# First layer by seven block products instead of eight, and the layers' side work ordered by a list scheduler

## The chip, the core and the metric

The kernel runs on one core of a Trainium2 chip. Four compute engines work side by side, each through its own instructions in order: TensorE (PE in the profile; its weight loads are a row of their own, PEld), VectorE (DVE), ScalarE (ACT) and GpSimd (POOL). SyncE (SP) issues most of the DMA transfers. The metric is the device time of one execution in microseconds, lower is better; the time before is the median of three runs, 629.89 us (629.33 to 630.28).

## The reference

```python
scores = (q @ k.T) / sqrt(64)                  # 4 batches x 12 heads, 448 x 448
scores = cap * tanh(scores / cap)              # cap = 30
attn = exp(scores - max); attn = attn / (attn.sum() + 1e-9)
x = (attn @ v)  -> (1792 tokens, 768)
h = x @ w_in                                   # 768 x 2048
g = where(h > 0, h, exp(min(h, 0)) - 1)
out = g @ w_out                                # 2048 x 768
```

All values are float32. The kernel writes each float32 factor as a high part in TensorE's `float32r` format plus a low part, and takes three products: high x high, high x low and low x high.

## The kernel before

Attention. Twelve rounds (`Attention.run`) handle 24 pairs of heads. Per round ScalarE runs seven `tanh` and seven `exp` passes over 128x896 elements, TensorE the scores, values and row sums, VectorE the casts, sums and evictions. `normalise` writes x, transposed: 128 of the 768 features by 448 tokens for each pair. `Tokens.high` and `Tokens.low` split x. The order of all this is written out by hand, as times in `AT` and `END`.

Layers. The 1792 tokens are cut into `BLOCKS` of 512, 512, 512 and 256. The 2048 hidden features are taken in `NR` = 8 rounds of two tiles of 128 (`FT` = 2). For each of the 32 units (round r, block t), `Moe.first` computes two hidden tiles (per tile 6 feature chunks x 3 products = 18 matmuls), and `Moe.second` multiplies the two activated tiles by the second weights into six output tiles (6 x 2 x 3 = 36 matmuls), in pairs of two PSUM banks. TensorE's order is: first layer of the next unit, then second layer of this one. So each unit has 72 matmuls, each round 288.

Work beside TensorE. `elu` (lines 240 to 256) takes a hidden tile through ScalarE `exp` (L245), VectorE `min` and add (L246), VectorE maximum and add (L249, reads PSUM), ScalarE copy into the high part (L254) and VectorE subtraction into the low part (L255). `finish` (L306) adds each pair of output tiles from PSUM to the accumulator in SBUF. In round 0 ScalarE copies them instead (L290). The weights arrive packed; `Weights.steps` unpacks each of the 32 tiles of 128x768 with three VectorE passes (L128 to L130), one ScalarE pass (L140), VectorE (L144), a GpSimd addition (L147), a ScalarE copy into the high part (L154) and a VectorE subtraction into the low part (L158). In the layers this runs as a string of steps at fixed places of each unit (`WRUN`), and mostly one step right behind the other.

Queues and buffers. VectorE, ScalarE and GpSimd run their instructions in the order written. PSUM has two single banks, `pv0` and `pv1`, for hidden tiles, and three pairs for outputs. SP's queue carries the weight loads (768 KB each) and, at the end, the output (512 KB each, smaller ones last).

Of the kernel before, what the change touches and what calls it, by code (L numbers as in the profile page):

```python
# [17 lines left out]
P = 128  # L18
# [9 lines left out]
NW = 2 * NF  # L28
CP = 64
WSTEPS = 5  # L30
# [9 lines left out]
def pieces(b):  # L40

    out = []
    for t, (t0, n) in enumerate(BLOCKS):
        lo, hi = max(t0, b * S), min(t0 + n, (b + 1) * S)
        if lo < hi:
            out.append((t, lo - t0, lo - b * S, hi - lo))
    return out

# [23 lines left out]
END = {  # L72
    "invert": 2.95, "spread": 2.97, "normalise": 3.2, "unit0": 0.1, "xh": 0.2, "elu0": 1.55, "unit0b": 1.6,
    "xl": 2.9, "elu1": 3.0,
    "weights": (1.0, 2.96, 3.25),
}
# [6 lines left out]
class Weights:  # L83
# [4 lines left out]
    def __init__(self, nc, pool, pre, w):  # L88
        self.nc, self.pool, self.pre, self.w = nc, pool, pre, w
        self.late = self.now = None  # L90
        self.scalar = False
        self.raw, self.split = {}, {}
        self.nraw = self.nmid = 0

    def buffer(self, k, n, width, dtype):

        if self.late and k % 2:
            return self.late.tile([P, width], dtype, name=f"{n}{k}", tag=n, bufs=1)
        if n == "wq":
            return self.pool.tile([P, width], dtype, name=f"{n}{k}", tag=n, bufs=1)  # L100
        at = 0 if n == "wr" else 2 * DM
        return self.pre[:, at : at + width].bitcast(dtype)

    def ahead(self):

        self.load(self.nmid + (2 if self.now is None else 1) - self.nraw)

    def load(self, n=1):
        for k in range(self.nraw, min(self.nraw + n, NW)):
            t = self.buffer(k, "wr", 2 * DM, I32)  # L110
# [4 lines left out]
    def steps(self):  # L115

        nc = self.nc
        k = self.nmid
        if k >= NW:
            return  # L120
        self.nmid += 1
        raw = self.raw.pop(k)
        high = raw.rearrange("p (n w) -> p n w", w=2)[:, :, 1]
        low = raw.bitcast(U16).rearrange("p (n w) -> p n w", w=4)[:, :, 1]
        v = self.buffer(k, "wv", DM, F32)
        q = self.buffer(k, "wq", DM, I32)
        vi = v.bitcast(I32)
        nc.vector.tensor_single_scalar(out=vi, in_=high, scalar=0x7FFFFFFF, op=ALU.bitwise_and)  # L128
        nc.vector.tensor_scalar_max(v, v, TINY)
        nc.vector.tensor_scalar(  # L130
# [8 lines left out]
        if self.scalar:  # L139
            nc.scalar.activation(out=q, in_=low, func=AF.Copy, scale=2.0**-13)  # L140
        else:
            nc.vector.tensor_scalar_mul(q, low, 2.0**-13)
        yield
# [5 lines left out]
        v = v.rearrange("p (c n) -> p c n", c=6)  # L149
        pool, n = (self.pool, 4) if k % 6 < 4 else (self.late, 2)  # L150
        h = pool.tile([P, 6, P], F32R, name=f"wh{k}", tag="wh", bufs=n)
        l = pool.tile([P, 6, P], F32R, name=f"wl{k}", tag="wl", bufs=n)
        if self.scalar:
# [5 lines left out]
        self.split[k] = (h, l)  # L159

    def run(self, n):

        for _ in range(n):
            if self.now is None:
                self.now = self.steps()
            if next(self.now, self) is self:
                self.now = None

    def get(self, f, second):
        return self.split[f // FT * 2 * FT + f % FT + FT * second]  # L170


class Tokens:


    def __init__(self, nc, pool, early):
        self.nc, self.pool, self.early, self.late = nc, pool, early, None
        self.x, self.parts = {}, {}

    def new(self, p):  # L180
        self.x[p] = self.pool.tile([P, BANK], F32, name=f"x{p}", tag="x", bufs=NPAIR + 1)[:, :S]
        return self.x[p]

    def split(self, p, t):
        self.high(p, t)
        self.low(p, t)

    def piece(self, p, t):
        return next((o, at, n) for k, o, at, n in pieces(p // PPB) if k == t)

    def high(self, p, t, vector=False):
        c = p % PPB
        o, at, n = self.piece(p, t)
        if (t, c) not in self.parts:
            n0 = BLOCKS[t][1]
            if t == NB - 1:
                both = self.late.tile([P, 2, n0], F32R, name=f"xb{c}", tag="xb", bufs=PPB)
                self.parts[t, c] = [both[:, 0], both[:, 1]]
            else:
                pool, k = (self.early, 2 * PPB) if t < 2 else (self.late, PPB)  # L200
                xh = pool.tile([P, BANK], F32R, name=f"xh{t}_{c}", tag="xh", bufs=k)[:, :n0]
                self.parts[t, c] = [xh, None]
        out, x = self.parts[t, c][0][:, o : o + n], self.x[p][:, at : at + n]
        if vector:
            self.nc.vector.tensor_copy(out=out, in_=x)
        else:
            self.nc.scalar.activation(out=out, in_=x, func=AF.Copy)

    def low(self, p, t):
        c = p % PPB  # L210
        o, at, n = self.piece(p, t)
        part = self.parts[t, c]
        if part[1] is None:
            part[1] = self.pool.tile([P, BANK], F32R, name=f"xl{t}_{c}", tag="x", bufs=NPAIR + 1)[:, : BLOCKS[t][1]]
# [568 lines left out]
```

## Time and profile before

| | us |
|---|---|
| median of three runs | 629.89 (629.33 to 630.28) |
| profiled execution, its own time | 629.86 |
| its span, first to last instruction | 627.6 |
| PE busy in the span | 618.4 (99%) |
| DVE busy | 444.4 (71%) |
| ACT busy | 282.9 (45%) |
| POOL busy | 62.3 (10%) |

A busy PE is not PE at its peak, because matmuls overlap: the distance between the starts of two matmuls (the pitch) tells what one costs in a stream. A share over the whole span mixes attention (to about 160 us) and the layers (from there on), so the views below are taken by stretch.

### The profile page before, as it was taken

What the parts mean: (1) busy time and instruction counts of PE and PEld (TensorE: products, weight loads), DVE (VectorE), ACT (ScalarE), POOL (GpSimd) and SP (SyncE); (2) the same over time, 40 slices, a digit from 0 to 9 for tenths busy, and PEclk for the clock granted to TensorE, in tenths of its full rate; (3) what the DMA queues carried; (4) which work ended last, traced back from release to release, by engine and by line L of the source; (5) the groups of instructions that cost most, each with busy time, mean ns of one, the idle gap of its engine ahead of it and who ended that gap; (6) DMA issues with size and microseconds to landing.
All of it is one profiled execution on the core that took longest, in us unless ns stands there. A gap on an engine that the chain in (4) does not pass through costs nothing.

```text
span 627.6 us, 8706 instructions
## 1 busy us (share of the span) xinstructions
PE 618.4 (99%) x3410; PEld 461.6 (74%) x3410; DVE 444.4 (71%) x672; ACT 282.9 (45%) x399; POOL 62.3 (10%) x40
## 2 busy tenths in 40 slices
PE   8999999999999999999999999999999999999996
PEld 3444444444788788888888888888888888888885
DVE  5898999998877556766776766576767577484443
ACT  6999999999445542222312222322332123121110
POOL 0010010010101211210111211111111121110000
PEclk9999999999999999999999999999999999999999
DMA  5546457561141311210211122111111122000224
GB/s 184 174 152 208 135 164 216 134 192 54 37 131 50 101 52 50 81 72 7 95 50 51 57 66 80 51 50 51 51 51 50 51 76 76 1 2 0 101 101 156
DMA packets 26227, 54.30 MB, mean 87 GB/s; under 512 B 9538, under 2 KB 13634, under 8 KB 26178
## 3 DMA queue, kind: packets, MB, share of 16 engines
q1 hardware_dynamic: 25890, 53.27, 26.7%
q8 instruction: 29, 0.48, 0.3%
q10 hardware_dynamic: 288, 0.39, 0.2%
q14 instruction: 20, 0.16, 0.1%
HBM read 47.97 MB, written 5.59 MB: 85 GB/s over the span
## 4 chain that ended last, share of the span: by engine, by line
PE 84%; DVE 9%; ACT 2%; DMA 2%; issue 1%; SPq 1%; POOL 1%; DVEq 0%; POOLq 0%; ACTq 0%
PE o L231 11%; PE o L232 11%; PE o L233 11%; PE h L231 11%; PE h L233 11%; PE h L232 11%; PE pv L414 7%; PE s L372 5%; DVE u L448 2%; PE sum L458 2%; PE pv L427 1%; PE s L389 1%; DVE xl L216 1%; DVE qkl L367 1%; DMA pre<-in_w_dram 1%
## 5 line engine op out<-in xcount | busy, mean ns | idle before, releaser
L231 PE MATMUL o<-gh,wh 128*128 128x512 f32 (+1 forms) x380 | 138.3, 364 | 0.4 <-ACT acc L290 0.4
L232 PE MATMUL o<-gl,wh 128*128 128x512 f32 (+1 forms) x380 | 138.2, 364 | 0.0
L233 PE MATMUL o<-gh,wl 128*128 128x512 f32 (+1 forms) x380 | 138.1, 363 | 0.0
L231 PE MATMUL h<-xh,wh 128*128 128x512 f32 x288 | 112.3, 390 | 0.1
L232 PE MATMUL h<-xl,wh 128*128 128x512 f32 x288 | 112.1, 389 | 0.0
L233 PE MATMUL h<-xh,wl 128*128 128x512 f32 x288 | 112.1, 389 | 0.0
L306 DVE TENSOR_TENSOR acc<-o,acc 128x1024 f32<-128x1024 f32 (+1 forms) x83 | 89.1, 1089 | 10.3 <-PE o L233 10.3
L254 ACT ACTIVATE gh<-e 128x512 fp32r<-128x512 f32 (+1 forms) x64 | 37.0, 579 | 103.8 <-DVE e L249 103.8
L245 ACT ACTIVATE e<-h 128x512 f32<-128x512 f32 (+1 forms) x64 | 34.6, 540 | 103.5 <-PE h L233 99.7
L231 PEld LDWEIGHTS o<-gh,wh 128*128 128x128 f32 x380 | 71.7, 189 | 12.4 <-ACT acc L290 0.9
L233 PEld LDWEIGHTS o<-gh,wl 128*128 128x128 f32 x380 | 71.7, 189 | 11.3
L232 PEld LDWEIGHTS o<-gl,wh 128*128 128x128 f32 x380 | 71.8, 189 | 11.2
L405 ACT ACTIVATE s<-s 128x896 f32<-128x896 f32 x84 | 76.6, 911 | 5.5 <-PE s L389 3.5
L407 ACT ACTIVATE p<-s 128x896 f32<-128x896 f32 x84 | 77.2, 919 | 2.7
L255 DVE TENSOR_TENSOR gl<-e,gh 128x512 fp32r<-128x512 f32 (+1 forms) x64 | 41.8, 653 | 41.3 <-ACT gh L254 40.6
L147 POOL TENSOR_TENSOR pre<-pre,wq 128x768 int32<-128x768 int32 x18 | 35.5, 1975 | 339.3 <-DVE pre L144 301.1
L246 DVE TENSOR_SCALAR e<-e 128x512 f32<-128x512 f32 (+1 forms) x64 | 26.4, 413 | 55.6 <-ACT e L245 55.5
L231 PEld LDWEIGHTS h<-xh,wh 128*128 128x128 f32 x288 | 54.1, 188 | 12.6 <-DVE e L249 0.9
L233 PEld LDWEIGHTS h<-xh,wl 128*128 128x128 f32 x288 | 54.1, 188 | 11.3
L232 PEld LDWEIGHTS h<-xl,wh 128*128 128x128 f32 x288 | 54.1, 188 | 10.9
L414 PE MATMUL pv<-p,vf 128*64 128x448 f32 x276 | 59.5, 552 | 0.2
L249 DVE SCALAR_TENSOR_TENSOR e<-h,e 128x512 f32<-128x512 f32 (+1 forms) x64 | 40.0, 625 | 2.2
(86 smaller groups left out, 722.9 us busy)
## 6 DMA issues: line engine op xcount, KB each, us to landing
pre<-in_w_dram SPq DMA_DIRECT2D x18, 768.0 KB, 4.5
wr<-in_w_dram SPq DMA_DIRECT2D x14, 768.0 KB, 4.2
raw<-in_qk_dram SPq DMA_DIRECT2D x22, 448.0 KB, 4.1
vf<-in_v_dram SPq DMA_DIRECT2D x23, 256.0 KB, 4.1
rb<-rec SPq DMA_DIRECT2D x48, 112.0 KB, 3.0
out_dram<-acc SPq DMA_DIRECT2D x9, 512.0 KB, 2.8
den<-sums SPq DMA_DIRECT2D x48, 1.8 KB, 1.9
out_dram<-acc SPq DMA_DIRECT2D x2, 256.0 KB, 3.5
```

The lines of the kernel that those rows point to most:

```text
L147: nc.gpsimd.tensor_tensor(out=vi, in0=vi, in1=q, op=ALU.add)
L231: mm(acc, wh[:, m, :], ph, start=first, stop=False)
L232: mm(acc, wh[:, m, :], pl, start=False, stop=False)
L233: mm(acc, wl[:, m, :], ph, start=False, stop=last)
L245: nc.scalar.activation(out=ev, in_=h, func=AF.Exp)
L249: nc.vector.scalar_tensor_tensor(out=ev, in0=h, scalar=0.0, in1=ev, op0=ALU.max, op1=ALU.add)
L254: nc.scalar.activation(out=gh, in_=ev, func=AF.Copy)
L255: nc.vector.tensor_tensor(out=gl, in0=ev, in1=gh.bitcast(F32), op=ALU.subtract)
L306: self.nc.vector.tensor_tensor(out=o, in0=s, in1=o, op=ALU.add)
L405: self.nc.scalar.activation(out=s, in_=s, func=AF.Tanh, scale=self.con.tanh_scale)
L407: self.nc.scalar.activation(out=pt, in_=s, func=AF.Exp, scale=self.con.exp_scale)
L414: self.nc.tensor.matmul(out[o, :S], w[j], x[j], **flags)
```

## The change

In rounds 1 to 7 the first layer for the last 1024 tokens is computed by Strassen's scheme. Two hidden tiles x 1024 tokens x 768 features is a 2x2 by 2x2 product of blocks (each 128 hidden features, 384 features deep, 512 tokens wide). Eight block products of 9 matmuls (3 chunks x 3 products) become seven. For it, four sums of weight quarters are formed each round (`Weights.sum`, `form_high`, `form_low`), and four sums of token quarters once, in place of x (`Tokens.combine`, 12 operations of 128x512). These are split into high and low parts in twelve chunks; nine chunks of 512 KB are sent to DRAM, and each round fetches 12 chunks back into a ring of three buffers (`NEXT` says which form follows which product). The seven products leave PSUM through one ScalarE copy (`keep`) and seven VectorE additions (`add`), which also combine them.

`BLOCKS` becomes 384, 384, 512, 512; the first two blocks are computed as before. The elu becomes two ScalarE passes (`Relu` with scale -1, `Exp` with scale -1) and one VectorE pass instead of one and two. The weights' first pass (L128) moves to ScalarE (`Abs`), and all raw tiles use one buffer. x becomes one tile, whose space later holds the accumulators.

The order of the work is no longer written by hand. `Plan` holds threads of `Step`s with an engine, a duration, a due time, and what each needs, gives, takes and frees. It runs them in simulated time; at each point the engine that is free first takes the step that is due first, and the instructions are emitted in this order. TensorE's order is fixed by `plan_products`. GpSimd and VectorE are independent engines in the plan. The normalisation of the last five pairs, with the DMAs around it, is dealt out by the plan too (`plan_rest`).

The core of the diff:

```diff
-BLOCKS = [(t, min(BANK, B * S - t)) for t in range(0, B * S, BANK)]
...
-WRUN = ((2, 2, 1, 1), (2, 2, 1, 1), (2, 1, 1, 1), (1, 1, 1, 1))
+BLOCKS = ((0, 384), (384, 384), (768, BANK), (768 + BANK, BANK))
...
+LAG = {"p": 0.15, "s": 0.1, "v": 0.06, "g": 0.1, "d": 1.8, None: 0.0}
+FREE = {"p": 0.0, "s": -3.7, "v": -0.75, "g": 1.2, "d": 0.0}
+NORMAL = 5
+NEXT = {6: (3, 0), 7: (4, 0), 4: (1, 0), 5: (2, 1)}
+USES = {6: 2, 7: 3, 4: 4, 5: 1}
+TAKES = {6: 2, 7: 3, 5: 1, 3: 4}
...
+        if scalar:
+            self.v[k] = self.v_buffer(k)
+            nc.scalar.activation(out=self.v[k], in_=high.bitcast(F32), func=AF.Abs)
+            yield
+            q = self.quotient(k)
+            nc.scalar.activation(out=q, in_=low, func=AF.Copy, scale=2.0**-13)
+            yield
+            v = self.v[k]
...
+    def sum(self, r, k):
+
+        a, b = (self.v[2 * FT * r + i].rearrange("p (j n) -> p j n", j=2) for i in range(FT))
+        x, y, op, o = (
+            (b[:, 0], b[:, 1], ALU.add, b[:, 1]),
+            (a[:, 0], b[:, 0], ALU.subtract, b[:, 0]),
+            (b[:, 1], a[:, 0], ALU.subtract, a[:, 0]),
+            (a[:, 1], a[:, 0], ALU.subtract, a[:, 1]),
+        )[k]
+        self.nc.vector.tensor_tensor(out=o, in0=x, in1=y, op=op)
...
+        self.nc.scalar.activation(out=h, in_=self.fresh[r, k], func=AF.Copy)
...
+        self.nc.vector.tensor_tensor(out=l, in0=self.fresh[r, k], in1=h.bitcast(F32), op=ALU.subtract)
...
+    def combine(self, i, k):
+
+        x = [[self.block(HC * j + i, PAIR + n) for n in range(2)] for j in range(2)]
+        o, a, b = (
+            (x[0][0], x[0][1], x[0][0]),
+            (x[0][1], x[1][1], x[0][1]),
+            (x[1][1], x[1][1], x[0][0]),
+            (x[1][0], x[1][0], x[1][1]),
+        )[k]
+        self.nc.vector.tensor_tensor(out=o, in0=a, in1=b, op=ALU.subtract)
...
+        self.nc.scalar.activation(out=t[:, 0], in_=self.form(n, i), func=AF.Copy)
...
+        self.nc.vector.tensor_tensor(out=l, in0=self.form(n, i), in1=h.bitcast(F32), op=ALU.subtract)
...
+        self.nc.sync.dma_start(out=d, in_=self.whole.pop((n, i)).bitcast(F32))
...
+        self.nc.sync.dma_start(out=t.bitcast(F32), in_=self.forms[n, i])
...
+            engine = min(first, key=lambda e: first[e])
+            now = first[engine]
+            due, _, step, head = min(
+                ((step.due, k, step, head) for k, (start, step, head) in enumerate(able)
+                 if step.engine == engine and start <= now),
+                key=lambda e: e[:2],
+            )
...
+        for step in order:
+            if step.f is not None:
+                step.f(*step.a)
...
+        self.nc.scalar.activation(out=e, in_=self.h[k], func=AF.Relu, scale=-1.0)
+        self.nc.scalar.activation(out=e, in_=e, func=AF.Exp, scale=-1.0)
...
+            out=e, in0=e, scalar=-1.0, in1=self.h.pop(k), op0=ALU.add, op1=ALU.max
...
+        a, b = {
+            1: ((0, 0), (0, 0)), 2: ((0, 1), (1, 0)), 3: (4, (1, 1)),
+            4: ((1, 1), 4), 5: (1, 1), 6: (2, 2), 7: (3, 3),
+        }[n]
...
+        u, out = {6: ("c1", "u2"), 7: ("u2", "u3"), 4: ("u3", "c"), 2: ("c1", None), 3: ("u2", None), 5: ("u3", None)}[n]
...
+        for t in range(2, NB):
+            self.plan_second(0, t - 2)
+            first(0, t)
+        self.plan_second(0, NB - 2)
+        for r in range(1, NR):
+            self.begun[r] = self.clock
+            for n in (1, 6):
+                if r == 1 and n == 1:
+                    first(r, 0)
+                self.plan_block(n, r)
+            if r > 1:
+                first(r, 0)
+            self.plan_second(r - 1, 3)
+            self.plan_block(7, r)
+            first(r, 1)
+            self.plan_second(r, 0)
+            for n in (4, 2, 3):
+                self.plan_block(n, r)
+            self.plan_second(r, 1)
+            self.plan_block(5, r)
+            self.plan_second(r, 2)
+        self.plan_second(NR - 1, 3)
+        self.plan.thread(*self.pe)
+
...
+        order = [(n, i) for i in range(HC) for n in (1, 4)] + [(n, i) for n in (3, 2) for i in range(HC)]
...
```

`plan_opening` gives the due times of the splits and sums in round 0: block 1 from -3.0, block 2 from 8, block 3 from 20, the sums from 24, the twelve chunks from 26 in steps of 1.4, in us from the start of the second hidden tile.

## Rows read from the trace of the kernel before

**Rows 1.** The page: granted TensorE clock in 40 slices, tenths of full speed.

```profile
PEclk9999999999999999999999999999999999999999
```

**Rows 2.** Stretches: start:end length, busy us (x instructions) per engine, clock, DMA share, GB/s.

```profile
323.20:380.80 57.60, 57.60 (x290) 49.15 (x289) 40.59 (x58) 15.28 (x25) 7.39 (x4) 1.00 0.17 55
...
163.80:210.00 46.20, 45.75 (x217) 38.29 (x218) 32.83 (x67) 22.28 (x42) 5.60 (x3) 1.00 0.30 89
```

**Rows 3.** TensorE in order of time: start, us, engine, line, tiles.

```profile
598.25 0.39 PE L231 MATMUL o<-gh,wh 128*128 128x512 f32 x1
...
598.48 0.39 PE L232 MATMUL o<-gl,wh 128*128 128x512 f32 x1
```

**Rows 4.** VectorE by line and shape, 170 to 627 us: xcount, busy us, mean ns.

```profile
L306 DVE TENSOR_TENSOR acc<-o,acc 128x1024 f32<-128x1024 f32 x63 | 75.9, 1218 | 9.4 <-PE o L233 9.4
...
L249 DVE SCALAR_TENSOR_TENSOR e<-h,e 128x512 f32<-128x512 f32 x47 | 32.5, 692 | 1.6
...
L158 DVE TENSOR_TENSOR wl<-pre,wh 128x768 fp32r<-128x768 f32 x15 | 14.3, 956 | 29.1 <-ACT wh L154 29.1
...
L144 DVE SCALAR_TENSOR_TENSOR pre<-pre 128x768 int32<-128x768 int32 x15 | 14.2, 946 | 0.0
...
L129 DVE TENSOR_SCALAR pre<-pre 128x768 f32<-128x768 f32 x14 | 7.8, 561 | 0.5
...
L249 DVE SCALAR_TENSOR_TENSOR e<-h,e 128x256 f32<-128x256 f32 x16 | 6.8, 425 | 0.6
```

**Rows 5.** ScalarE by line and shape, the same stretch.

```profile
L254 ACT ACTIVATE gh<-e 128x512 fp32r<-128x512 f32 x47 | 29.7, 632 | 72.7 <-DVE e L249 72.7
...
L245 ACT ACTIVATE e<-h 128x512 f32<-128x512 f32 x46 | 27.4, 597 | 88.8 <-PE h L233 88.8
...
L154 ACT ACTIVATE wh<-pre 128x768 fp32r<-128x768 f32 x15 | 12.7, 844 | 62.1 <-POOL pre L147 33.6 <-PE h L232 28.6
...
L140 ACT ACTIVATE wq<-pre 128x768 int32<-128x768 uint16 x14 | 12.6, 899 | 0.0
```

**Rows 6.** All groups by line: the one table load of ScalarE.

```profile
L636 ACT ACT_TABLE_LOAD x1 | 1.3, 1283 | 1.1 <-PEq L772 1.1
```

**Rows 7.** Timelines of POOL and DVE around two GpSimd additions.

```profile
346.15 1.85 POOL L147 TENSOR_TENSOR pre<-pre,wq 128x768 int32<-128x768 int32 x1 [14.24 <-DVE pre L144]
...
346.69 1.59 DVE L246 TENSOR_SCALAR e<-e 128x512 f32<-128x512 f32 x1 [0.69 <-ACT e L245]
...
374.09 2.35 DVE L306 TENSOR_TENSOR acc<-o,acc 128x1024 f32<-128x1024 f32 x2
...
374.31 1.85 POOL L147 TENSOR_TENSOR pre<-pre,wq 128x768 int32<-128x768 int32 x1 [13.19 <-DVE pre L144]
```

**Rows 8.** What VectorE waited for, 208 to 540 us: total us, times, longest.

```profile
DVE e L246 <- ACT e L245: 39.8, 29, 3.2
...
DVE wl L158 <- ACT wh L154: 34.7, 17, 5.9
...
DVE gl L255 <- ACT gh L254: 30.3, 47, 0.7
```

**Rows 9.** Chain that ended last, in order of time: start, us, what.

```profile
89.71 0.91 PE pv L427 x8
...
102.25 0.91 PE pv L427 x8
...
153.49 0.91 PE pv L427 x8
```

**Rows 10.** VectorE by line and shape, 0 to 170 us.

```profile
L216 DVE TENSOR_TENSOR xl<-x,xh 128x64 fp32r<-128x64 f32 x6 | 1.0, 208 | 0.0
```

**Rows 11.** DMA issues: xcount, KB each, median us from issue to landing.

```profile
wr<-in_w_dram SPq DMA_DIRECT2D x14, 768.0 KB, 4.2
...
out_dram<-acc SPq DMA_DIRECT2D x2, 256.0 KB, 3.5
...
out_dram<-acc ACTq DMA_DIRECT2D x1, 128.0 KB, 2.6
```

More of the change, by code (lines that the diff above doesn't have):

```diff
@@ L177, in __init__ @@
         self.nc, self.pool, self.early, self.late = nc, pool, early, None
-        self.x, self.parts = {}, {}
+        self.all = pool.tile([P, NC, B * S], F32, name="x")
+        self.parts = {}
+        self.forms, self.ring, self.whole = {}, {}, {}
     def new(self, p):
[L181 to L189, printed above, removed]
@@ L209, in low @@
[L209 to L214, printed above, removed]
-        h, l = (a[:, o : o + n] for a in part[:2])
-        self.nc.vector.tensor_tensor(out=l, in0=self.x[p][:, at : at + n], in1=h.bitcast(F32), op=ALU.subtract)
+        b, c = divmod(p, PPB)
+        return self.all[:, c, b * S : b * S + S]
@@ new lines, in block, with high @@
+    def block(self, c, t, n=1):
+        t0, width = BLOCKS[t]
+        return self.all[:, c : c + n, t0 : t0 + width] if n > 1 else self.all[:, c, t0 : t0 + width]
+    def high(self, c, t, vector=False):
+        width = BLOCKS[t][1]
+        if t == 1:
+            part = self.parts[1, c]
+        elif t == PAIR + 1 and c < HC:
+            part = [self.spare[:, (2 * c + i) * BANK : (2 * c + i + 1) * BANK] for i in range(2)]
+        else:
+            pool, n, bufs = (self.early, "x", NC) if t == 0 else (self.late, "b", 3 * HC)
+            part = [pool.tile([P, width], F32R, name=f"x{i}{t}_{c}", tag=n + i, bufs=bufs) for i in "hl"]
+        self.parts[t, c] = part
+        if vector:
+            self.nc.vector.tensor_copy(out=part[0], in_=self.block(c, t))
+        else:
+            self.nc.scalar.activation(out=part[0], in_=self.block(c, t), func=AF.Copy)
@@ new lines, in plan_first @@
+    def plan_first(self, r, t, i):
+        f, end = r * FT + i, 0.0
+        bank = ("h", r, t, i)
+        for c in range(NC):
+            more = {"takes": ("bank", bank)} if c == 0 and (r, t) != (0, 0) else {}
+            needs = [("w", self.tile(f, 0))] + [("x", t, c)] * (t > 0)
+            if c == NC - 1:
+                more["gives"] = ("p", r, t, i)
+            end = self.product(self.hidden, r, t, i, (c,), n=3, width=BLOCKS[t][1], needs=needs, **more)
+        frees = (bank,) if (r, t) != (0, 0) else ("h0",) if i else ()
+        self.plan_elu(r, t, i, end, needs=(("p", r, t, i),), frees=frees)
@@ L726, in path, with pool @@
[L726 to L729 removed]
+                def pool(kind, on=ctx, **more):
+                    return on.enter_context(tc.tile_pool(name=f"{kind}{tag}", bufs=1, **more))
+                x.dr = dr = pool("dr", space=DRAM)
+                tail, at, heads = (ctx.enter_context(ExitStack()) for _ in range(3))
+                back = pool("tail", tail, side="right")
```

687 lines of the change are left out of this document (497 added, 190 removed).

## Prediction

> **What bounds the kernel now.** I read three views, in this order. The stretches come first. In one round's length of the layers, 323.2 to 380.8 us, TensorE is busy 57.60 of 57.60 us with 290 matmuls (a round has 288), at clock 1.00 [rows 2], which is the upper of its two levels, 2.4 GHz; it stays there in every slice [rows 1]. A busy TensorE proves little by itself, so the second view is TensorE in order of time. Two matmuls 512 wide start 0.23 us apart although each is shown as 0.39 us long [rows 3]. One round of 57.6 us gives the finer figure: 216 matmuls of 512 and 72 of 256, on average 448 wide, make 57.6 / 288 = 0.200 us each. That is 448 / 2400 = 0.1867 plus 0.0133 us. So 512 wide costs 0.2267 us, 256 wide 0.120, and 384 wide, which the trace does not show, 0.1733 by the same line. TensorE is at its column rate: in the layers, a matmul taken away is time taken away, as long as nothing else comes late. The third view is the other engines in the same round: VectorE 40.59 us, ScalarE 15.28, GpSimd 7.39 [rows 2]. VectorE has 17 us of room, and most of this is waiting in its own order: 105 us in the 332 us from 208 to 540, behind ScalarE passes [rows 8].
>
> **What TensorE loses and keeps.** Before, the two wide blocks of the new cut would cost 2 tiles x 2 blocks x 6 chunks x 3 = 72 matmuls a round in the first layer. Seven products of 9 are 63. Nine matmuls of 512 go, in seven rounds: 63 x 0.2267 = 14.28 us. The new cut itself (384, 384, 512, 512) keeps the number of matmuls and the mean width 448, so it costs nothing. A new round is 57.6 - 2.04 = 55.56 us of TensorE.
>
> **VectorE and ScalarE in a new round.** VectorE, by rows 4, with 128x384 taken as 0.56 us between 0.425 (256) and 0.692 (512): four weight tiles lose L128 and keep 0.561 + 0.561 + 0.946 + 0.956 = 3.02 each, 12.1 us. Four weight sums and four low parts of 384 are 8 x 0.56 = 4.5. The elu keeps its maximum and low part, four tiles of 512 and four of 384: 8 x 0.69 + 8 x 0.56 = 10.0. Accumulation is 6 x 1.218 and 6 of 768 wide at about 0.95, 13.0. Seven additions of products are 4.8. The sum is 44.4 of 55.56 us (80%), against 40.6 of 57.6 (70%). ScalarE [rows 5]: tiles 4 x (0.84 + 0.90 + 0.84) = 10.3, four high parts of weight sums 2.0, three passes for eight elu tiles 13.2, the kept product 0.6, together 26 us (47%). `Relu` and `Abs` are not in the trace. The nearest rows are `Exp` (0.597) and `Copy` (0.632) of the same shape; the upper bound is one table load of 1.283 each [rows 6], which with loads to and fro at 12 places a round would be 31 us more and fill ScalarE. I take no load, because `Exp`, `Tanh` and `Copy` already share the one load of the whole trace. The Trainium skill, "ScalarE: Activation LUTs", section "Table sets: the hidden batching unit", says that cheap functions such as relu and abs lie in every set; no row here shows it.
>
> Where could a round lose? Two single PSUM banks serve eleven tiles a round. Products 4, 2, 3 follow each other at 2.04 us; product 3 needs the bank of 4, so VectorE has 2.04 us for one addition of 0.69 and whatever it is in the middle of (up to 1.22). That fits, with 0.1 us to spare. I put 0.1 us on each of seven rounds, 0.7 us in all, bounds 0 and 4.
>
> **The opening (round 0).** Here the new work is bunched. From the start of the second hidden tile, TensorE reaches product 6 of round 1, the first that needs sums, after 3.12 + 6.24 + 6.24 + 8.16 + 6.24 + 8.16 + 8.16 + 6.24 + 2.04 = 54.6 us. Until then VectorE must do: low parts of x 6 x 0.56 + 12 x 0.69 = 11.6; five normalisations and the row sums 4.1; eight elu tiles 4 x 1.12 + 4 x 1.38 = 10.0; token sums 12 x 0.69 = 8.3; their low parts 8.3; one weight low part 0.96 and two tiles 6.0; weight sums and one low part 2.8. That is 52.1 us. Back to back, two accumulations of 1.218 take 2.35 [rows 7], so each of some 60 operations gives back about 0.08, and 47 to 48 us remain. That leaves 6 to 7 us for waiting. In the like stretch before, 163.8 to 210 us, VectorE stood idle 46.2 - 32.8 = 13.4 us [rows 2], by waits of the kinds of rows 8, at steps placed right behind the one they wait for; the new order can put other ready work between.
>
> GpSimd takes some of the rest. While its addition ran (346.15 to 348.00), a VectorE pass that began at 346.69 took 1.59 us and ended at 348.28, where even the two-operand maximum of this width takes 0.692 [rows 4, 7]. While another ran (374.31 to 376.16), two accumulations that read PSUM went at full speed [rows 7]. So an addition holds up some VectorE work by 0.9 to 1.85 us. Three fall into the opening (2.7 to 5.6 us), four into each round (3.6 to 7.4), and the plan counts the two engines as independent. The Trainium skill, "SBUF — State Buffer", section "Who interferes with whom", states the rule: a VectorE operation with two SBUF inputs, or in a two-port mode, and a GpSimd operation that reads SBUF exclude each other for a whole instruction. By that rule nearly all new work (sums, low parts) is of the exposed kind; the two cases in the trace agree with it.
>
> The balance is 47.5 + 4 = 51.5 us of work for 54.6, so 3 us for waits. I take a TensorE stall of 2.0 us, bounds 0 (waits mostly gone) and 9 (waits as before: 51.5 + 13.4 - 54.6 = 10, of which a little is hidden behind product 6).
>
> **DMA.** Each round now fetches 12 chunks of 512 KB beside four weight loads. A load of 768 KB lands in 4.2 us [rows 11], so three chunks, even one after the other at that price, land in 12.6 us. The shortest gap is from product 4 to product 5: 2 x 2.04 + 6.24 = 10.3 us, plus 1.4 from chunk one's release to the end of product 4, plus 1.4 until chunk three is used: 13.1. I take 0 us; with a weight load ahead in SP's queue the group would be 3.7 us late.
>
> **Attention.** Up to its eighth round a round takes 102.25 - 89.71 = 12.54 us, the last four (153.49 - 102.25) / 4 = 12.81 [rows 9]. These four lose 1.1 us in all. The new cut takes VectorE work out of them: the 64-token pieces of x out of three of these rounds (two splits of 0.2 us per round and part [rows 10]). I take -0.8 us, bounds 0 and -1.1.
>
> **The end.** The last addition is 512 wide instead of 256: 0.69 for 0.425 us. The last transfers are 256 KB (3.5 us) instead of 128 KB (2.6) [rows 11]. Together 0.3 to 1.2; I take +0.7.
>
> **The sum.** The profiled execution took 629.86 us (span 627.6 and 2.3 around it), the median of the runs is 629.89, so one base serves: 629.86 - 14.28 - 0.8 + 2.0 + 0.7 + 0.7 = 618.2 us.
>
> **The rivals.**
> 1. VectorE's opening is late by the full 9 to 10 us, with the additions of GpSimd in it, and rounds lose up to 4: 629.86 - 14.28 + 9 + 4 + 0.7 = 629, or half of it 622 to 625. For: work of 51.5 for 54.6 us, tight. Against: waits of the old kind are what a scheduler removes.
> 2. By the rule on shared ports alone: the rounds too lose what each addition holds up. 44.4 + 7.4 = 51.8 us stays under 55.56, so the rounds hold, and the opening takes its 5.6 instead of 4: 620 us.
> 3. A fetch group queued behind a weight load is late by 3.7 us in each of seven rounds: 618.2 + 26 = 644, or 622 for one round. Against: a weight load fits between the groups.
> 4. Slower than before: VectorE keeps waiting in its order as now. Rows 8 give 105 us in 332, that is 18.2 us a round. 44.4 + 18.2 = 62.6 us would make VectorE the bound of each round, 5.0 above the old 57.6: 629.86 + 35 = 665 us. It decides from 13.2 us of waits a round. Against: waits for `exp` and for high parts end when other ready work is put in front.
> 5. The change doesn't do what it says: 384-wide matmuls cost as much as 512. Then 8 x 144 x 0.053 = 61 us are lost. Against: a straight line through 256 and 512.
>
> **How the numbers follow.** A measurement of this kernel can tell about 0.2% (1.3 us) from no change. Forecast with its small terms, 614.5 to 621: 0.65 (rival 2's 620 us lies in it, with 0.15 of this). Rival 1: 0.18, two thirds of it below 626. Rival 3: 0.06. Rival 4: 0.08. Rival 5 and others: 0.03. The low end is all terms at their best: 629.86 - 14.28 - 1.1 + 0.3 = 614.8, rounded to 614.5. The high end, 626, takes in 0.65 + 0.12 + 0.03 = 0.80. Faster by over 0.2%: 0.65 + 0.16 + 0.04 + 0.01 = 0.86. Within: 0.03. Slower: 0.11.
>
> **What would show it right or wrong.** In the changed kernel's stretches a middle round should take 55.6 to 55.9 us, with TensorE at 63 matmuls fewer in all, VectorE near 44 us busy (less what overlaps) and its waits well under 13. What TensorE waits for should be a few us in all, most of it at the first matmuls of product 6 in round 1, released by VectorE or ScalarE work on the sums. VectorE passes over SBUF should be 1 to 2 us long beside GpSimd additions. It would be wrong if TensorE waits in every round (banks, or a DMA into the ring), if a table load stands beside `Relu`, or if the granted clock fell to its lower level after a stall.

## The result, and the profile after

The changed kernel takes 623.45 us (median of 4 runs, 622.50 to 623.72) where the kernel before took 629.61 beside it (4 runs): a ratio of 0.9898, 95% interval 0.9881 to 0.9915. The forecast was 618.2 us with a range of 614.5 to 626. Sign and range held; 5 us of the gain are missing. The profiled execution of after took 623.72 us, its span is 621.9.

The stretches come first, as in rows 2: start:end, length, busy us (instructions) of PE, PEld, DVE, ACT and POOL, granted clock, DMA share, GB/s. The first line has the length of a round and lies in round 2 and the start of round 3, the second is round 1, the third a piece of the opening with the start of round 1.

```profile
276.50:332.44 55.94, 55.94 (x281) 50.32 (x280) 46.20 (x62) 25.56 (x42) 8.05 (x5) 1.00 0.49 169
...
209.26:272.36 63.10, 58.34 (x280) 51.28 (x279) 50.87 (x74) 38.08 (x60) 11.82 (x6) 0.97 0.64 225
...
171.00:221.00 50.00, 47.05 (x234) 41.74 (x232) 47.37 (x73) 36.19 (x62) 6.13 (x3) 1.00 0.46 164
```

The starts of TensorE's rounds lie at 209.26 (round 1), 272.36, 328.30, 384.23, 440.16, 496.10 and 552.03 us. So round 1 takes 63.10 us and every later one 55.93; a round before took 57.64 by the same landmarks. In rounds 2 to 7 TensorE waits for nothing. In the layers it waits four times in the whole trace (us in total, times, longest):

```profile
PE o L402 <- ACT wv L118: 1.8, 1, 1.8
PE m L402 <- issue: 1.7, 1, 1.7
...
PE m L402 <- DVE e L435: 1.2, 1, 1.2
PE h L402 <- DVE e L435: 0.8, 1, 0.8
```

The wait of the last line, at 163.76 us (1.0 us lost), was there before the change as well. The other three lie in round 1. Here they are one by one, in order of time (start, us, engine, line, tiles, idle before and releaser). The first is at product 1:

```profile
212.38 0.62 ACT L276 ACTIVATE t<-x 128x512 fp32r<-128x512 f32 x1
212.90 1.01 ACT L467 ACTIVATE x<-o 128x1024 f32<-128x1024 f32 x1
213.91 0.63 ACT L276 ACTIVATE t<-x 128x512 fp32r<-128x512 f32 x1
214.44 0.89 ACT L121 ACTIVATE wq<-pre 128x768 int32<-128x768 uint16 x1
215.24 0.47 ACT L430 ACTIVATE e<-h 128x384 f32<-128x384 f32 x1
...
216.30 0.55 DVE L435 SCALAR_TENSOR_TENSOR e<-e,h 128x384 f32<-128x384 f32 x1
...
216.91 0.50 PE L402 MATMUL m<-xh,wh 128*128 128x512 f32 x1 [1.21 <-DVE e L435]
```

Product 1 needs the PSUM bank of the first hidden tile of round 1. That tile was complete at about 212.4 us; its bank is freed by the maximum at L435, which ends at 216.85. In between ScalarE, in its fixed order, did 2.8 us of other work (two chunks' high parts, a copy out of PSUM, a weight step) before the tile's first pass at 215.24. The second wait follows at product 6:

```profile
217.89 2.11 POOL L148 TENSOR_TENSOR wv<-wv,wq 128x768 int32<-128x768 int32 x1 [13.46 <-DVE wv L145]
...
218.24 2.18 DVE L449 TENSOR_TENSOR gl<-e,gh 128x384 fp32r<-128x384 f32 x1
...
218.86 0.39 PE L404 MATMUL m<-xh,wl 128*128 128x512 f32 x1
...
220.34 0.54 DVE L435 SCALAR_TENSOR_TENSOR e<-e,h 128x384 f32<-128x384 f32 x1
...
220.98 0.47 PE L402 MATMUL m<-t,forms 128*128 128x512 f32 x1 [1.74 <-issue]
```

The subtraction at L449 took 2.18 us beside the GpSimd addition; without one such a pass takes 0.55. The maximum that frees the bank of the second hidden tile stood behind it, ended at 220.88, and TensorE went on at 220.98. The trace names no releaser ("issue"); that it is this bank is read from the order and the 0.1 us between the two. The third wait, for a pair of banks of the second layer, and what came after it:

```profile
254.99 1.85 POOL L148 TENSOR_TENSOR wv<-wv,wq 128x768 int32<-128x768 int32 x1 [7.54 <-DVE wv L145]
...
255.34 1.92 DVE L211 TENSOR_TENSOR forms<-pre,forms 128x384 fp32r<-128x384 f32 x1
...
261.39 0.95 DVE L472 TENSOR_TENSOR x<-o,x 128x768 f32<-128x768 f32 x1
...
262.48 0.47 PE L402 MATMUL o<-gh,wh 128*128 128x512 f32 x1 [1.81 <-ACT wv L118]
...
263.09 0.63 PE L404 MATMUL o<-gh,wl 128*128 128x512 f32 x1
263.52 0.63 PE L402 MATMUL o<-gh,wh 128*128 128x512 f32 x1
```

The pair's tiles were complete at about 254.2 us; the accumulation at L472 that frees them ended at 262.34, behind a queue that again held a stretched pass (1.92 us). The ScalarE pass that the row names (L118) had nothing to do with these banks. After the wait eight matmuls stand 0.43 us apart instead of 0.23. The granted clock had fallen to the lower of the two levels, 1.2 GHz, with TensorE busy (columns as in the stretches above):

```profile
262.95:266.30 3.35, 3.35 (x9) 2.57 (x9) 3.31 (x6) 1.42 (x3) 0.00 (x0) 0.50 0.61 213
```

From the wait's end at 262.48 to 266.43 us the slow matmuls cost 1.7 us more than the pitch of 0.228. The three waits cost 1.39, 1.89 and 1.97 us; with the slow matmuls that is 6.9 of the 7.17 us by which round 1 is longer than its followers. The rest stands at the first matmuls behind the first two waits.

Four lines of the page and of the lines' view, for the terms of DMA and the table load (columns as in rows 11 and 6). All twelve chunks are sent to DRAM, not the nine that the description of the change names:

```profile
t<-form SPq DMA_DIRECT2D x81, 512.0 KB, 5.3
pre<-in_w_dram SPq DMA_DIRECT2D x32, 768.0 KB, 5.7
...
form<-t SPq DMA_DIRECT2D x12, 512.0 KB, 3.9
...
L1098 ACT ACT_TABLE_LOAD x1 | 1.3, 1283 | 1.1 <-PEq L1249 1.1
```

And the chain that ended last, in attention, to be read against the last line of rows 9:

```profile
152.50 0.91 PE pv L866 x8
```

### The profile page after: what moved, and what is told of

Its sections match the earlier page's. It is cut to its first block, busy times and chain, and to the rows that moved or that the text cites. A ratio compares the mean times of both kernels' runs of the same rounds, so it can differ in the third digit from the quotient of the medians.

```text
span 621.9 us, 8936 instructions
## 1 busy us (share of the span) xinstructions
PE 608.4 (98%) x3347; PEld 473.6 (76%) x3347; DVE 491.0 (79%) x684; ACT 365.3 (59%) x527; POOL 63.7 (10%) x40
## 4 chain that ended last, share of the span: by engine, by line
PE 87%; DVE 7%; DMA 2%; ACT 2%; issue 1%; SPq 0%; DVEq 0%; ACTq 0%
PE o L404 11%; PE o L402 11%; PE o L403 11%; PE pv L853 10%; PE s L811 8%; PE m L402 5%; PE m L404 5%; PE m L403 5%; PE h L402 5%; PE h L403 5%; PE h L404 5%; PE sum L897 3%; PE pv L866 2%; PE s L828 1%; DVE xl L248 1%
## 5 line engine op out<-in xcount | busy, mean ns | idle before, releaser
L402 PE MATMUL o<-gh,wh 128*128 128x384 f32 (+1 forms) x380 | 138.2, 364 | 1.8 <-ACT wv L118 1.8
L404 PE MATMUL o<-gh,wl 128*128 128x384 f32 (+1 forms) x380 | 138.4, 364 | 0.0
L403 PE MATMUL o<-gl,wh 128*128 128x384 f32 (+1 forms) x380 | 138.0, 363 | 0.0
L472 DVE TENSOR_TENSOR x<-o,x 128x768 f32<-128x768 f32 (+1 forms) x83 | 89.8, 1084 | 22.6 <-PE o L404 22.0
L148 POOL TENSOR_TENSOR wv<-wv,wq 128x768 int32<-128x768 int32 x24 | 47.3, 1973 | 362.6 <-DVE wv L145 322.9
L402 PE MATMUL h<-xh,wh 128*128 128x384 f32 (+1 forms) x210 | 71.4, 340 | 0.8 <-DVE e L435 0.8
L404 PE MATMUL h<-xh,wl 128*128 128x384 f32 (+1 forms) x210 | 71.2, 339 | 0.0
L403 PE MATMUL h<-xl,wh 128*128 128x384 f32 (+1 forms) x210 | 71.2, 339 | 0.0
L445 ACT ACTIVATE gh<-e 128x384 fp32r<-128x384 f32 (+1 forms) x64 | 36.0, 570 | 27.1 <-DVE e L435 27.1
L430 ACT ACTIVATE e<-h 128x384 f32<-128x384 f32 (+1 forms) x36 | 18.0, 499 | 54.8 <-PE h L404 54.7
L435 DVE SCALAR_TENSOR_TENSOR e<-e,h 128x384 f32<-128x384 f32 (+1 forms) x36 | 20.2, 564 | 34.4 <-ACT e L431 34.3
L449 DVE TENSOR_TENSOR gl<-e,gh 128x384 fp32r<-128x384 f32 (+1 forms) x64 | 41.0, 650 | 6.7 <-ACT gh L445 6.7
```

Of the source, the lines that this page charges most:

```text
L148: nc.gpsimd.tensor_tensor(out=vi, in0=vi, in1=q, op=ALU.add)
L402: mm(acc, wh[:, m, :], ph, start=first, stop=False)
L403: mm(acc, wh[:, m, :], pl, start=False, stop=False)
L404: mm(acc, wl[:, m, :], ph, start=False, stop=last)
L435: self.nc.vector.scalar_tensor_tensor(out=e, in0=e, scalar=-1.0, in1=self.h.pop(k), op0=ALU.add, op1=ALU.max)
L445: self.nc.scalar.activation(out=self.g[k][0], in_=self.e[k], func=AF.Copy)
```

## The experiments

All twelve were timed beside the kernel before; ratios are to it, with 95% intervals. The theory (T1) is that round 1 loses because VectorE's and ScalarE's queues are overfull from the opening into round 1. The rivals are: GpSimd's hold-ups are the price, the token sums or the DMA of the ring are, or the new rounds are slow in themselves.

**start2: Strassen from round 2 on.** Round 1 stays plain, so the token sums have a round more, and the weight sums of round 1 fall away.

```diff
+START = 2
...
-        for r in range(1, NR):
+        for r in range(1, START):
+            self.begun[r] = self.clock
+            for t in range(NB):
+                first(r, t)
+                self.plan_second(*((r - 1, 3) if t == 0 else (r, t - 1)))
+        for r in range(START, NR):
```

> The seven products begin in round 2; round 1 computes its first layer as the kernel before does (18 matmuls more of 512 in the first layer than a Strassen round... 72 against 63, so 9 more, 2.04 us). The changed kernel loses 7.2 us of TensorE time in its first Strassen round (209.3 to 272.4 us lasts 63.1 us, later rounds 55.93). Theory 1 (the sums' VectorE work, bunched before round 1 and held up by GpSimd additions, makes the first Strassen round late): with a round of 57.6 us more until the sums are needed the waits of 1.4, 1.9 and 2.0 us and the slow clock behind them go, TensorE waits under 1.5 us after 165 us, and the time is 623.45 - 7.2 + 2.0 = 618.3 us (617.5 to 619.5). Rival (each first Strassen round pays for its start, wherever it lies): the waits move one round on, 624 to 626 us.

Measured: 618.34 us (618.17 to 618.74), ratio 0.9821 (0.9805 to 0.9837): faster than the changed kernel by 5.1 us with one Strassen round fewer. TensorE's waits in the layers are down to the old one:

```profile
PE h L403 <- DVE e L436: 0.8, 1, 0.8
...
326.70:382.60 55.90, 55.90 (x280) 50.31 (x279) 43.91 (x59) 25.36 (x41) 7.56 (x4) 1.00 0.50 170
```

The books close to 0.4 us: 7.17 us of round 1's excess saved and 57.64 - 55.93 = 1.71 given up make 5.46. The loss belongs to starting in round 1, not to the scheme, and it does not move on to round 2, as the rival had it.

**plan_only: no Strassen round, no sums and no ring.** The new cut, the scheduler, the new elu and the weights' `Abs` alone (START = 8, the chunks and token sums not planned).

> No Strassen round at all, no sums, no ring: the new cut, the elu with Relu, Abs on ScalarE and the list scheduler alone. Theory 1 (these parts are neutral but for the relief of attention): TensorE does 288 matmuls in each of eight rounds, 57.6 us each, attention is 1.0 us shorter as in the changed kernel, so 628 to 629.2 us. Rival (the scheduler's order or the ScalarE passes cost time by themselves, and the first Strassen round only shows it): over 631 us, with TensorE waits of several us in round 1.

Measured: 629.52 us (629.30 to 629.88), ratio 0.9998 (0.9988 to 1.0008). By itself the rest of the change is worth nothing (the theory's 628 to 629.2 us is missed by 0.3), with VectorE down from 40.59 us a round [rows 2] to 35.00:

```profile
267.12:324.92 57.80, 57.80 (x290) 52.06 (x288) 35.00 (x44) 23.13 (x36) 7.38 (x4) 1.00 0.17 55
```

A round takes 57.80 us, 0.16 more than before with the same number of matmuls and no wait; over eight rounds these 1.3 us eat up what attention gains. So a slightly greater pitch comes with the new cut even without Strassen; where it stands is read under the pitch, below.

**no_combine: the twelve token sums left out.** The chunks split x itself.

```diff
     def combine(self, i, k):
...
-        self.nc.vector.tensor_tensor(out=o, in0=a, in1=b, op=ALU.subtract)
+        pass
```

> The twelve VectorE sums of token quarters (128x512, 8.3 us in all) are left out, so the forms are plain quarters of x; everything else, the twelve chunks, their high and low parts, the sends and the fetches, stays. Theory 1 (VectorE's amount of work sets the waits of round 1): round 1 shrinks from 63.1 to 56 to 58 us, the time is 617.5 to 619.5 us. Rival 2 (the ring: a chunk's slot comes free only when its send has landed, 3.9 us median, and this holds ScalarE's queue and all behind it): waits stay, 622.5 to 624 us.

Measured: 623.44 us (622.38 to 623.46; the changed kernel 623.45): 8.3 us of VectorE work less, no gain. Waits of 0.82, 1.89 and 1.97 us and the slow matmuls remain. T1, told as an amount of work in the opening, falls. The sums stood between 186.5 and 198.7 us, the order behind them is fixed, and the gap opens there: ScalarE holds a chunk's high part behind a `Relu` (L430) and an `Exp` that wait for TensorE, and VectorE idles:

```profile
197.24 0.60 ACT L430 ACTIVATE e<-h 128x512 f32<-128x512 f32 x1 [2.90 <-PE h L404]
...
199.06 0.69 DVE L282 TENSOR_TENSOR t<-x,t 128x512 fp32r<-128x512 f32 x1 [4.23 <-ACT t L276]
```

**narrow_add: the GpSimd additions cut to 16 of 768 columns.**

```diff
-        nc.gpsimd.tensor_tensor(out=vi, in0=vi, in1=q, op=ALU.add)
+        nc.gpsimd.tensor_tensor(out=vi[:, :16], in0=vi[:, :16], in1=q[:, :16], op=ALU.add)
```

> Each GpSimd addition covers 16 of 768 columns (the other columns of the weights lack their lowest bits), so GpSimd is busy some 0.1 to 0.3 us per tile instead of 1.85. Theory 1 with the hold-ups: three VectorE operations in the stretch to 262 us lose their excess (two low parts at 183.1 us took 2.94 instead of 1.3, the low part at 218.2 us took 2.18 instead of 0.55, the one at 255.3 us 1.92 instead of 0.55), the second and third of these stood right ahead of TensorE's waits; together 3 to 5 us: 618.5 to 620.5 us, and no VectorE operation of 128x384 over 0.8 us. If the hold-ups are not on the path: 622.5 to 623.7 us.

Measured: 619.99 us (619.31 to 621.17), ratio 0.9850 (0.9834 to 0.9867): 3.5 us better. The subtraction that took 2.18 us takes 0.58, and the second wait shrinks from 1.89 to 0.30 us:

```profile
218.60 0.51 POOL L148 TENSOR_TENSOR wv<-wv,wq 128x16 int32<-128x16 int32 x1 [17.20 <-DVE wv L145]
...
218.94 0.58 DVE L449 TENSOR_TENSOR gl<-e,gh 128x384 fp32r<-128x384 f32 x1
```

The third wait falls from 1.97 to 0.66 us, and here the trace names L472 itself as its releaser; no run of slow matmuls follows. The first grows from 1.39 to 2.25: ScalarE has the same order there as in the changed kernel, with one more wait of 0.42 us for a send, and the tile's first pass begins at 215.94 instead of 215.24.

**start2_narrow: both together.** 

> Strassen from round 2 on, and each GpSimd addition cut to 16 of its 768 columns (the rest of the weights' low bits is left out). In start2 (618.34 us) TensorE waited nowhere after 163.8 us. If the hold-ups by GpSimd cost time only where the opening and round 1 are overfull, nothing is left to gain here: 618.0 to 618.6 us. If they still cost in the plain rounds, by stalls too short to be seen singly, the rounds of 55.93 us shrink and the time falls by 1 us or more.

Measured: 618.49 us (618.20 to 618.68), ratio 0.9824 (0.9808 to 0.9841), the same as start2. So the hold-ups cost where the queues are full, and nothing that can be measured in the other rounds, though in the changed kernel two or three stretched passes stand in each of them (four additions).

**elu_first: the elu of round 1's first block due 20 us earlier.**

```diff
-        self.plan_elu(r, t, i, end, needs=(("p", r, t, i),), frees=frees)
+        self.plan_elu(r, t, i, end - 20.0 * ((r, t) == (1, 0)), needs=(("p", r, t, i),), frees=frees)
```

> All work stays; only the due times of the elu of round 1's first block are 20 us earlier, so ScalarE and VectorE take its steps ahead of the chunks' high parts and the weights. Theory 1 (the two PSUM banks wait behind the chunks in the queues): the waits ahead of products 1 and 6 (1.4 and 1.9 us) go or move by at most 1 us to the last chunk of the ring; 620 to 622 us. If the ring's chunks are the true limit: product 6 waits as long for its form, 623 to 624.5 us.

Measured: 624.79 us (624.02 to 626.48), in neither theory's range. The two waits for PSUM banks at products 1 and 6 are gone. In their place product 6 waits 0.91 us at its last chunk, for a low part of the token sums (L282), and product 7 waits 0.41 us for a fetched chunk. One wait of 4.7 us stands further on, for a low part (L449) behind a stretched pass of 2.15 us, followed by slow matmuls:

```profile
PE o L403 <- DVE gl L449: 4.6, 1, 4.6
...
PE m L403 <- DVE t L282: 0.6, 1, 0.6
PE m L402 <- DMA t<-form: 0.3, 1, 0.3
```

What is put in front pushes something else back. One item's due time doesn't mend it.

**no_fetch: the 81 fetches left out**; products 4 to 7 read what the ring last held. And **no_store: the sends left out too.**

```diff
# no_fetch and no_store
-        if i == 0:
-            self.ring[n] = []
-        t = self.chunk(f"{r}_{n}", i)
-        self.nc.sync.dma_start(out=t.bitcast(F32), in_=self.forms[n, i])
-        self.ring[n].append((t[:, 0], t[:, 1]))
+        self.ring[n] = self.ring[2]
...
# no_store
-        self.nc.sync.dma_start(out=d, in_=self.whole.pop((n, i)).bitcast(F32))
+        self.whole.pop((n, i))
```

> The 81 fetches of 512 KB are left out: the three chunks of the ring stay as they are, and products 7, 4 and 5 of each round use the form that product 6 should have; the twelve sends stay. In the changed kernel matmuls of 512 that read the ring follow each other at 0.2328 us, the other products at 0.2283, against 0.2269 in the kernel before, and a round takes 55.93 us where 55.56 were forecast. Theory A (transfers into SBUF beside the matmuls slow them a little): pitches go back to 0.227 and a round to 55.6 us, 6 x 0.35 = 2 us less: 621.3 us, and the weight loads land in 4.2 to 4.5 us instead of 5.7. Theory B (it is where the ring's operands lie or what they hold): 0.2328 stays, rounds 55.9, 623 to 623.7 us.

> Sends and fetches are both left out: a ring slot is free as soon as its low part is written. Theory 1 (ScalarE's fixed order: the high part of a chunk waits for its slot, that is for a send to land, and Exp and Relu of round 1's first tiles stand behind it in the queue, so their PSUM banks come free late): the wait ahead of product 1 (1.4 us) goes, that ahead of product 6 shrinks by as much as ScalarE is earlier; against the run without fetches 1.5 to 3.5 us less. Rival (GpSimd and VectorE alone): the same time as without fetches.

Measured: 625.71 us (624.57 to 627.03) without the fetches, slower than with them; 623.23 (622.38 to 624.21) without the sends as well. Rounds 2 to 7 take 55.93 us in no_fetch too, with the ring's pitch unchanged, though a weight load now lands in 4.3 us instead of 5.7: the 42 MB of fetches cost nothing there. In the profiled execution (627.03 us, the slowest of four that lie at 624.6 and 626.7 to 627.0) product 1 waits longer, with slow matmuls behind it (waits, then the stretch 219 to 226 us, clock 0.54):

```profile
PE m L398 <- DVE e L431: 4.0, 1, 4.0
PE o L398 <- ACT wv L118: 1.8, 1, 1.8
...
219.00:226.00 7.00, 6.40 (x16) 4.75 (x17) 5.52 (x8) 3.53 (x7) 2.11 (x1) 0.54 0.73 239
```

The missing fetches do not explain this. The instructions of ScalarE, VectorE and GpSimd stand in the same order as in the changed kernel, and there the first fetch is issued only at 221.95 us. What differs is when transfers landed ahead of product 1. ScalarE, in that order, waited 1.27 us for a weight load and 0.32 and 0.83 us for sends, 2.4 us in all, and the tile's first pass began at 217.93 us instead of 215.24:

```profile
210.31 0.91 ACT L118 ACTIVATE wv<-pre 128x768 f32<-128x768 f32 x1 [1.27 <-DMA pre<-in_w_dram]
...
217.93 0.47 ACT L426 ACTIVATE e<-h 128x384 f32<-128x384 f32 x1
```

The slowest of the sends issued from 203 to 214 us took 4.0 us to land in the changed kernel, 5.7 in no_fetch and 6.2 in narrow_add. Why they differ is open. So the first wait depends on when transfers land, in one and the same order. Without the sends it is 1.96 us, where the theory had it gone; the sends and loads lengthen it, but they are not its cause.

**start2_h0: start2 with the two first hidden tiles in PSUM tiles of their own**, so that the first is free before the second is done.

```diff
-        t = self.ps.tile([P, 2, BANK], F32, name="h0", tag="s", bufs=3)
         for i in range(FT):
-            self.h[0, 0, i] = t[:, i, : BLOCKS[0][1]]
+            t = self.ps.tile([P, 2, BANK], F32, name=f"h0{i}", tag="s", bufs=3)
+            self.h[0, 0, i] = t[:, 0, : BLOCKS[0][1]]
```

> As the run that begins Strassen in round 2, with the first two hidden tiles in two PSUM tiles instead of the halves of one. In all kernels so far the second hidden tile waited some 0.9 us until VectorE had read the first (its neighbour bank in the same tile). Theory (this wait is made by the tile, not by the work ahead): it goes, 618.3 - 0.9 = 617.4 us. If the row sums ahead of it need the time anyway: 618.3 us.

Measured: 618.10 us (617.89 to 618.34), ratio 0.9819 (0.9803 to 0.9836). The old wait at 163.8 us moves to 165.3 and shrinks from 1.0 to 0.56 us (now for the sums' eviction, L920). The gain is within what two measurements differ by.

**The pitch: start2_resident, start2_pad, start2_swap.** In all rounds from 2 on, a matmul that reads the ring has a pitch of 0.2329 us (mean distance of starts, 153 of them from 285 to 520 us), one of the other products 0.2283. In start2_resident products 4 to 7 read a resident part of x in place of the ring (token sums left out, the fetches stay). In start2_pad a small unused tile moves the ring by 576 bytes of each partition. In start2_swap the ring and the split x that product 3 reads change places.

```diff
# start2_resident
-        q = (lambda: x.ring[b]) if isinstance(b, int) else (lambda: x.quarter(*b))
+        q = (lambda: x.quarter(0, 0)) if isinstance(b, int) else (lambda: x.quarter(*b))
# start2_pad
+                    nc.vector.memset(x.back.tile([P, 144], F32, name="pad"), 0.0)
# start2_swap
+        elif t == PAIR + 1:
+            whole = self.back.tile([P, 2, BANK], F32R, name=f"x{t}_{c}", tag="ring", bufs=HC)
+            part = [whole[:, 0], whole[:, 1]]
...
-        return self.back.tile([P, 2, BANK], F32R, name=f"t{n}_{i}", tag="ring", bufs=HC)
+        return self.late.tile([P, 2, BANK], F32R, name=f"t{n}_{i}", tag="ring", bufs=HC)
```

> Strassen from round 2 on; products 4 to 7 read x of the first 384 features and the third block (resident buffers) in place of the token sums in the ring, so their values are left out; the fetches still run. A matmul that read the ring had a pitch of 0.2329 us, other products 0.2283. If the ring's place or the way it is written makes it slower, products 4 to 7 come down to 0.228 and a round to 55.93 - 36 x 0.0046 = 55.76 us, the whole 617.3 us. If it is the products themselves (their waits, or their PSUM bank), the pitch stays at 0.2329 and the time at 618.3.

> Strassen from round 2 on, correct; the ring's three buffers lie 576 bytes of each partition lower, by a small unused tile beside them (one extra VectorE memset). If the pitch of 0.2329 us hangs on the address at which the ring stands, it changes here; if it is the data or the fetch that makes the ring slower, it stays at 0.2329 and the time at 618.3 us.

> Strassen from round 2 on, correct; the ring changes places with the split x that product 3 reads (the last three feature chunks of the fourth block: the same 12 KB of each partition, at the right end of the buffers). If the place makes the slower pitch, products 4 to 7 fall to 0.228 us a matmul and product 3, which then reads the old place, rises to 0.233: a round of 55.93 - 36 x 0.0046 + 9 x 0.0046 = 55.81 us. If it is how the ring is filled and reused (token sums written and sent, fetched by DMA), product 3 stays at 0.228, products 4 to 7 at 0.233, the round at 55.93 and the whole at 618.3 us.

Measured: start2_resident 617.52 us (617.40 to 617.70), rounds of 55.76, the products at 0.2279 on average. start2_pad 618.48 (618.19 to 619.31), the ring still at 0.2329. start2_swap 617.93 (617.79 to 618.03), ratio 0.9818 (0.9802 to 0.9835), rounds of 55.79, the ring at 0.2288 and product 3 up from 0.227 to 0.233. First and last matmul of product 6 (reads the ring) and of product 3 in one round of start2_swap:

```profile
341.62 0.39 PE L406 MATMUL m<-t,forms 128*128 128x512 f32 x1
...
343.43 0.39 PE L408 MATMUL m<-t,forms 128*128 128x512 f32 x1
...
360.29 0.39 PE L406 MATMUL m<-x,forms 128*128 128x512 f32 x1
...
362.15 0.39 PE L408 MATMUL m<-x,forms 128*128 128x512 f32 x1
```

Eight steps take 1.81 us there and 1.86 us here. In the changed kernel it is the other way about, 1.87 us for product 6 and 1.82 for product 3:

```profile
290.94 0.39 PE L402 MATMUL m<-t,forms 128*128 128x512 f32 x1
...
292.81 0.39 PE L404 MATMUL m<-t,forms 128*128 128x512 f32 x1
...
309.69 0.39 PE L402 MATMUL m<-xh,forms 128*128 128x512 f32 x1
...
311.51 0.39 PE L404 MATMUL m<-xh,forms 128*128 128x512 f32 x1
```

So the slower pitch belongs to the place at the right end of the buffers, whoever lies there: not to the fetch (no_fetch kept it), not to the data (no_combine, whose chunks hold plain x, has 0.2329 too), not to a shift of 576 bytes. What it is about that place stays open.

These means hide a second effect, which has nothing to do with the ring. A stream of one width away from that place settles at 0.2267 us for 512 columns. The excess over that stands in the first nine matmuls behind a change of width from 384 to 512. In plan_only, which has no ring, the first, tenth and nineteenth matmul behind such a change begin at:

```profile
273.38 0.39 PE L403 MATMUL o<-gh,wh 128*128 128x512 f32 x1
...
275.46 0.39 PE L403 MATMUL o<-gh,wh 128*128 128x512 f32 x1
...
277.50 0.39 PE L403 MATMUL o<-gh,wh 128*128 128x512 f32 x1
```

Nine steps take 2.08 us, the next nine 2.04. The changes from 512 to 384 cost some 0.03 us each. Three of either kind in a round of plan_only make 0.20 us, against 0.04 at the changes of 256 and 512 in the kernel before: that is the whole difference of 57.80 and 57.64. Products 4 and 5, which follow work of 384 columns, therefore stay at 0.231 in start2_resident and start2_swap, while 6 and 7 fall from 0.233 to 0.227.

Of the kernels that do the whole computation start2_swap has the lowest time, 1.8% below the kernel before and 5.5 us below the changed one; start2_h0, 0.2 us behind it, can't be told from it.

## Why the prediction was right and wrong

Its sum against the trace, term by term, in us:

| term | forecast | measured | from |
|---|---|---|---|
| 63 matmuls fewer | -14.28 | -14.3 | pitch before 0.2269 |
| attention | -0.8 | -1.0 | 152.50 for 153.49 [rows 9] |
| opening and round 1 | +2.0 | +7.2 | 63.10 - 55.93 |
| seven rounds | +0.7 | +2.3 | 7 x (55.93 - (57.64 - 2.04)) |
| end | +0.7 | +0.1 | last matmul's start to the span's end, 5.97 for 5.85 |
| outside the span | 0 | -0.4 | 1.8 for 2.3 |

The measured column sums to -6.1; the profiled executions differ by 629.86 - 623.72 = 6.14.

**What bounds the kernel: right.** TensorE at its column rate, matmuls taken away are time taken away; 384 wide costs 0.1733 to 0.1737 us against the line's 0.1733. Rival 5 (a poor rate at 384) is out by this.

**VectorE and ScalarE in a round: right.** VectorE 46.20 us in the stretch shown and 44.51 from 328.30 to 384.23 us (forecast 44.4), ScalarE 25.56 and 25.35 (26). Rival 4, waits as before that would make VectorE the bound (665 us), is out: TensorE waits nowhere in rounds 2 to 7.

**No table load: right.** One ACT_TABLE_LOAD in the trace, as in rows 6, with `Relu` and `Abs` in it. The Trainium skill, "ScalarE: Activation LUTs", section "Table sets: the hidden batching unit", has such functions in every set; this trace agrees.

**DMA at 0: right.** A chunk lands in 5.3 us and a weight load in 5.7, later than the 4.2 of rows 11, yet in rounds 2 to 7 no matmul waits for a fetch, and rival 3 is out. In the opening transfers did matter, which no term held: ScalarE waited 0.98 us for a send in the changed kernel, and 2.4 us for a weight load and two sends in no_fetch.

**The opening: the failed step.** The step reads "The balance is 47.5 + 4 = 51.5 us of work for 54.6, so 3 us for waits. I take a TensorE stall of 2.0 us". The balance itself came close: from 171 to 221 us VectorE was busy 47.4 of 50 us, hold-ups included, a share of 95% where the forecast's 51.5 of 54.6 is 94%. What failed is the step from the balance to the stall. It priced a late arrival of the sums at product 6, where only 1.9 of the 5.3 us of waits stand. None of the three waits is for a sum (a wait of that kind, 0.91 us, showed only in elu_first, with the others out of its way); all three are for PSUM places that VectorE frees, with the freeing instruction standing in its place of a fixed queue, behind a ScalarE order in one case and behind a pass stretched by GpSimd in the others. With little slack the queue's order decides, and not the amount of work further up: taking 8.3 us out there gained nothing (no_combine), moving one item moved the wait (elu_first), and taking the hold-ups out gained 3.5 us (narrow_add). Second, the count stopped at product 6. The full queue went on, and the third wait, at 262 us, lies 41 us beyond the end of the count. Third, the slow matmuls (1.7 us) were named among the signs of being wrong, and came, but had no price. Rival 1 in its half form (622 to 625 us) is what happened, by another mechanism in detail: its price was for a late opening, and it included losses in the later rounds, which have no waits. So the time lies in the range because the range made room for a late opening, not because the stall was foreseen. The other terms nearly cancel by luck: +1.6 us in the rounds against -1.2 in attention, at the end and outside the span.

**Rival 2, the rule on shared ports.** The hold-ups are as the forecast described them: 2.18 and 1.92 us for passes of 0.55 beside GpSimd additions. The Trainium skill, "SBUF — State Buffer", section "Who interferes with whom", gives the rule; the trace and narrow_add agree with it. By the lines of VectorE from 272 to 540 us the rounds have the stretched passes too (xcount, busy us, mean ns):

```profile
L211 DVE TENSOR_TENSOR forms<-pre,forms 128x384 fp32r<-128x384 f32 x10 | 13.8, 1378 | 0.0
...
L449 DVE TENSOR_TENSOR gl<-e,gh 128x384 fp32r<-128x384 f32 x20 | 11.0, 551 | 3.8 <-ACT gh L445 3.8
```

Its forecast that the rounds hold all the same and only the opening pays is borne out by start2_narrow; its time of 620 us was too low, since a delay in the queue came out as waits at two places and as slow matmuls (3.5 us by narrow_add), and the first wait is none of GpSimd's making.

**The rounds: a mis-sized term.** Forecast 0.1 us each for PSUM banks, and there is no such wait; found 0.33 each, all of it pitch. Of this 0.17 us is the ring's place (55.93 against 55.76 in start2_resident, where no product reads it), and 0.16 the new cut (57.80 in plan_only against 57.64), of which the prediction says that it keeps the mean width, "so it costs nothing". I had taken the pitch from one round and let it hold for tiles anywhere and for any order of widths.

**The end: too high.** I charged the wider last addition and transfer at full price; the trace shows 0.1 us.

## What to carry to other kernels

Where side work is bunched to within a few per cent of the time that is there, don't turn the leftover into a stall by subtraction: look for the instructions that free PSUM or a buffer for the bounding engine, and count what stands ahead of each in its engine's order, past the first deadline too. A costly set-up can be worth a plain round more: starting the cheaper scheme one round later gave up 1.7 us and saved 7.2, 5.1 us net as measured. A stretched pass costs only where its engine has no slack, so the same hold-up can be worth 3.5 us in one stretch and nothing in the next.

## What the runs showed of the hardware that was not expected

- In a stream of its own width a matmul of 512 columns had a pitch of 0.233 us when its moving operand lay in the 12 KB of each partition at the right end of the buffers, and 0.227 from other places (start2_swap), independent of the data, of DMA into it and of a shift by 576 bytes.
- Nine steps behind a change from 384 to 512 columns took 2.08 us, the next nine 2.04 (plan_only).
- With TensorE otherwise busy all the time, a wait of 1.97 us was followed by eight matmuls 0.43 us apart (clock 0.50 from 262.95 to 266.30 us); in narrow_add a wait of 2.25 us was not followed by any (clock 1.00 from 217 to 222 us), nor in no_store one of 1.97 us ahead of the very same matmul (clock 1.00 from 260 to 268 us). The length of the wait alone does not decide, and the 1.7 us are not its fixed price.
- A subtraction of 128x384 with both operands in SBUF took 2.18 us beside a GpSimd addition of 128x768 (2.11 us), and 0.58 us beside one of 16 columns.
